# Gates on ScalarE, a second routing with PSUM operands, and weight decoding moved into the last stage

## The chip, the cores and the metric

The kernel runs on one core of one Trainium2 chip, as one program. The metric is the device time of one launch in microseconds (us); lower is better. The kernel before takes 538.42 us, the median of three runs (537.2 to 539.23). The core's engines are TensorE (PE in the profile, its weight loads PEld), VectorE (DVE), ScalarE (ACT), GpSimd (POOL) and SyncE (SP), which here only issues DMAs.

## The reference

Three blocks follow each other, all in float32:

```python
# 1. attention: B=2, H=8, S=576, D=64
scores = (1/sqrt(D)) * rotate(q) @ rotate(k).T      # rotary embedding
attn = exp(scores - max); attn /= sum(attn) + 1e-9
x = (attn @ v)  reordered to (1152 tokens, 512)

# 2. routed experts: 8 experts, 512 -> 1024 -> 512, one expert per token
logits = x @ w_gate + modality_bias[modality_id]
e_idx = argmax(logits); gate_w = softmax(logits)[e_idx]
out[mask] = gate_w[mask] * (relu(x[mask] @ w1[e]) @ w2[e])      # for each expert e

# 3. dense block: 512 -> 2048 -> 512
h = out @ w_in
y = (h * tanh(softplus(h))) @ w_out
```

## The kernel before, in words

**Precision.** Products are made in a reduced float format with a correction: each operand is split into a high part (ScalarE copies it, for instance `whi`, `xh`, `hh`, `w2h`) and a low part (VectorE or POOL subtracts: `wlo`, `xl`, `hl`, `w2l`), and each product takes three matmuls: high by high, high by low, low by high.

**Attention** handles the 16 heads in an order that a planner (`Plan`) writes out ahead of time from estimated durations. Its X tiles collect the attention output per token; `LG` collects the gate logits of each head.

**Routing** (`routing(b, bank)`) runs once for each half of the tokens (b = 0, 1): a long chain of small VectorE operations turns the logits into the expert of each token, its place among the tokens of that expert, the table of the expert tiles (`tbl`, `te`) and the number of extra tiles (`nx`). Each token's row, with its gate value in an extra column, is scattered to DRAM by five indirect DMAs on POOL. For b = 0 the chain is interleaved with attention, and its intermediate results lie in a corner of a PSUM bank (`side`, `near`, `cur["rtile"]`); for b = 1 it runs after attention, and they lie in SBUF. `merge_extra` then joins the two tables of extra tiles, and `nx` is loaded into a register on the engines (`values_load`).

**Expert stage.** Four main tiles, (0, 0), (0, 1), (1, 0), (1, 1), of 304 tokens each. `moe_g` multiplies a tile's rows by their gates (line 630), `moe_x` transposes them on TensorE and splits them, and `moe_tile` makes eight products of the first matrix (12 matmuls each; ScalarE writes `hh`, VectorE `hl`, line 706) and four of the second (24 matmuls each; ScalarE writes Y, line 731). The next tile's gates are issued at the start of the second matrix, its transposes after the second of these four products. The tile's weights come in eight chunks through SP's queue (line 577), are split by ScalarE (line 585) and POOL (line 590), and a chunk is loaded when an older one has been split. A loop over extra tiles, which runs zero or more times, stands between the first two tiles and the last two.

All of this is written as generators, which yield ahead of each operation the engine and an estimated duration; for TensorE each matmul is one yield. Their consumers set the order. While routing 1 runs, `pump` issues an amount of expert matmuls for each VectorE yield of the routing, and afterwards `drive` steps through the rest and slips in a decode step at every so-many yields:

```python
if y[0] == "dve":
    pump(P["rq"][(i > 9) + (i > 20)])        # P["rq"] = (0.45, 0.47, 0.2)
...
nq_[0] += 1                                   # one TensorE yield
if nq_[0] % (3 * every) == 0:                 # every = P["dec"][0..2]
    decode(1, limit)
```

**Decoding.** The last stage's weights (16 blocks, f = 0 to 15, each 128 x 1024) come as 64-bit words, 1 MB per block, and three VectorE integer operations per block rebuild the 32-bit values (lines 1188, 1193, 1198). After a block's third step the load of block f + 2 is issued on SP's queue (line 1181; there are two buffers). Near the end of tile (0, 1) a "quiet" mark stops decoding for 48 yields.

**Last stage.** The dense block takes the token columns in two groups, first 640 columns in two pieces of 320, then 512 in two pieces of 256. For each of 16 weight blocks and each piece there is one unit `h` (12 matmuls, line 1346), then tanh, square and copy on ScalarE, a reciprocal (line 1368) and a product (line 1369) on VectorE, a high part on ScalarE and a low part on POOL (line 1386), and the output products `o` (line 1403). The three PSUM banks of `h` are reused in turn, so a unit waits for the line-1369 product of the third unit before it. What is not yet decoded is decoded here, in a fixed place about four units ahead of its use:

```python
m = 2 * q
if q < FC2:
    for z in range(3):
        at2(m - 4.05 + 0.6 * z, lambda n=3 * q + z + 1: decode(n - nd[0]))
```

`decode` does nothing for steps that are done. [...]

Of the kernel before, what the change touches and what calls it, by code (L numbers as in the profile page):

```python
# [10 lines left out]
F32 = mybir.dt.float32  # L11
F32R = mybir.dt.float32r
I32 = mybir.dt.int32
AF = mybir.ActivationFunctionType
ALU = mybir.AluOpType
AX = mybir.AxisListType
PSUM = bass.MemoryType.PSUM
# [3 lines left out]
DM = H * D  # L21
# [7 lines left out]
XC = DM  # L29
# [6 lines left out]
FC2 = F2 // 128  # L36

Q = {'r0': 2.45, 'rd': 2.0, 'tanh': 1.06, 'rec': 1.1, 'hi': 2.2, 'lo': 2.38, 'o': 3.86}
P = {'sd': (3,), 'dl': (10, 20), 'qd': (2, 3), 'alt': (0.1, 4), 'd0': 41, 'vl': 9, 'c': (-145.0, 22.5, -2.0), 'w3': 3, 'rq': (0.45, 0.47, 0.2), 'dec': (5, 5, 5), 'rl': 3, 'ah': 0, 'eps': 0.05, 'slack': 0.1}
K = {'ld': -22.67, 'prep': (-24.92, -22.38, -23.33, -27.14, -20.49, -7.62), 'sc': (-8.42, -3.18, 1.68, 1.67, 2.84, 10.44, 1.99, 8.05, 9.75), 'max': (-2.26, -5.46, -1.21, -1.85, 5.06, 8.41, 4.71, 11.42, 13.72), 'exp': (-3.19, 1.66, 6.32, 3.7, 13.26, 11.14, 14.6, -2.87, 25.74), 'tr': (0.69, 2.1, 2.56, 2.68, 5.53, 7.5, 8.45, 9.85, 10.88, 11.85, 15.56, 16.66, 16.92, 19.98), 'hi': (-3.91, -0.31, 2.51, 3.62, 4.25, 4.9, 5.01, 5.32, 7.26, 9.77, 13.56, 14.12, 14.6, 15.66), 'lo': (0.77, 1.83, 5.61, 6.34, 6.67, 7.32, 10.02, 10.73, 12.18, 13.92, 13.94, 14.62, 17.33, 18.02), 'pv': (7.08, 7.84, 10.5, 10.69, 14.13, 14.25, 14.32, 15.96, 18.04, 20.31, 21.03, 22.86, 23.97, 25.61), 'evac': (14.53, 9.65, 6.27, 25.13), 'rec': (-4.7, -0.45, 4.11, 12.71), 'fmm': (4.53, -3.79, 16.24, 17.22), 'norm': (15.5, 16.11, 26.18, 35.69)}  # L40

QT = [(0, 128), (128, 128), (256, 64), (320, 128), (448, 128)]
# [31 lines left out]
class Plan:  # L74
# [39 lines left out]
    def pick(self, e):  # L114
        best, lines = None, set()
        for o in self.todo[e][:40]:
# [8 lines left out]
            if best is None or t < best[0] - 1e-9:  # L125
                best = (t, o)
            if t <= self.free[e] + P["eps"]:
                break
# [40 lines left out]
    def run(self):  # L169
# [3 lines left out]
        while any(self.todo.values()):  # L173
            best = None
            for e in self.todo:
                c = self.pick(e)
                c = c and (c[0], 1, c[1])
                for o in self.alt[e][:4]:
# [4 lines left out]
                    t = max(t, self.free[e])  # L183
                    if (c is None or t + o[4] - P["alt"][0] <= c[0]) and t + o[4] + P["alt"][1] < end:
                        c = (t, 1, o)
                for st in self.streams:
                    if st["next"][0] != e:
                        continue
                    t = self.start(st)
                    if c is None or t + (st["next"][1] - P["slack"] if e in st["low"] else 0.0) <= c[0]:  # L190
                        c = (t, 0, st)
# [19 lines left out]
def moe_kernel(ctx: ExitStack, tc: tile.TileContext, aps, out):  # L211
    nc = tc.nc
# [87 lines left out]

    regs = {}
    tbl = {}
    scat, nxs, tes = [], [], []

    def routing(b, bank):
        t = lambda sh, nm, dt=F32: rp.tile(sh, dt, tag=nm, name=f"{nm}{b}")
        side = b == 0
        room = [0]

        def near(sh, nm):  # L310


            if not side:
                return t(sh, nm)
            n = 1
            for x in sh[1:]:
                n *= x
            o = room[0]
            room[0] += n
            v = cur["rtile"][0:sh[0], o:o + n]  # L320
            if len(sh) == 3:
                v = v.rearrange("p (a b) -> p a b", b=sh[2])
            return v

        V = nc.vector
# [4 lines left out]
            out=lg, in_=LG[b].rearrange("p j h e -> p j e h"),  # L330
# [15 lines left out]
            out=val, in0=lg, scalar=0.0, in1=iota8[:, 0:1, :].to_broadcast(sh),  # L346
            op0=ALU.is_ge, op1=ALU.mult,
# [46 lines left out]
        if not side:  # L394
# [8 lines left out]
            out=pos, in_=pz.rearrange("p (e j) -> p j e", j=5), axis=AX.X, op=ALU.add  # L403
# [5 lines left out]
        for j, (_, qn) in enumerate(QT):  # L409
            yield "pool", 1.07, False  # L410
            sc = nc.gpsimd.indirect_dma_start(
                out=scratch, out_offset=bass.IndirectOffsetOnAxis(ap=row[:qn, j:j + 1], axis=0),
                in_=X[b][:qn, j], in_offset=None,
# [9 lines left out]
        n0 = t([1, NE], "n1")  # L423
# [5 lines left out]
            out=n1, in0=ce, scalar=float(T), in1=n0, op0=ALU.is_gt, op1=ALU.add  # L429
        )  # L430
        if side:
# [5 lines left out]
            out=qi, data0=n1, data1=zero[0:1, :NE], initial=0.0, op0=ALU.add, op1=ALU.add  # L437
# [7 lines left out]
            out=st, in0=s0, scalar=float(-T), in1=base[0:1, 0:n:5], op0=ALU.mult, op1=ALU.add  # L445
# [5 lines left out]
            out=nx, in0=qi[:, NE - 1:NE], scalar1=-2.0, scalar2=None, op0=ALU.add  # L451
        )
        tv = iotat[0:1, 0:ns]
        if b:
# [3 lines left out]
                out=tv[:, 0:2], in0=iotat[0:1, 0:2], scalar1=nx, scalar2=None, op0=ALU.add  # L458
# [3 lines left out]
                out=tv[:, 2:ns], in0=iotat[0:1, 2:ns], scalar1=nxs[0], scalar2=-2.0,  # L462
                op0=ALU.subtract, op1=ALU.add,
# [3 lines left out]
        if side:  # L467
# [4 lines left out]
            out=lt, in0=qi[:, None, :].to_broadcast(s8),  # L472
            in1=tv[:, :, None].to_broadcast(s8), op=ALU.is_le,
        )
        te = t([1, ns, 2], f"te{b}")
        tm = near([1, ns, 2], "tm") if side else te
# [7 lines left out]
            out=lt, in0=iota8[0:1, 0:1, :].to_broadcast(s8),  # L484
            in1=e8[:, :, None].to_broadcast(s8), op=ALU.is_equal,
# [8 lines left out]
            out=cs, in0=tv, scalar=float(T), in1=cs, op0=ALU.mult, op1=ALU.add  # L494
# [4 lines left out]
            out=tm[:, :, 1], in0=cs, scalar1=s1, scalar2=o1, op0=ALU.mult, op1=ALU.add  # L499
# [3 lines left out]
            out=tm[:, :, 1], in0=tm[:, :, 1], scalar1=0.0, scalar2=float(ROWS - T),  # L503
            op0=ALU.max, op1=ALU.min,
# [3 lines left out]
            out=tm[:, :, 0], in0=tm[:, :, 0], scalar1=float(NE - 1), scalar2=None, op0=ALU.min  # L508
        )
        if side:  # L510
            yield "dve", 0.12, True
            V.tensor_copy(te, tm)
        tes.append(te)
        tbl[b] = ti = const.tile([1, 2, 2], I32, name=f"tbl{b}")
        yield "dve", 0.12, True
        V.tensor_copy(ti, te[:, 0:2])

    def merge_extra(nx):

        V = nc.vector  # L520
        n0, n1 = NS[0] - 2, NS[1] - 2
        sh = [1, n0, 2]
        m = rp.tile([1, n0], F32, tag="mm", name="mm")
        yield "dve", 0.12, True
        V.tensor_scalar(
            out=m, in0=iotat[0:1, 0:n0], scalar1=nxs[0], scalar2=None, op0=ALU.is_lt
        )
        d = rp.tile(sh, F32, tag="md", name="md")
        yield "dve", 0.12, True
        V.tensor_tensor(out=d, in0=tes[0][:, 2:], in1=tes[1][:, 2:2 + n0], op=ALU.subtract)  # L530
        yield "dve", 0.12, True
        V.tensor_tensor(out=d, in0=d, in1=m[:, :, None].to_broadcast(sh), op=ALU.mult)
        yield "dve", 0.12, True
        V.tensor_tensor(
            out=tes[1][:, 2:2 + n0], in0=tes[1][:, 2:2 + n0], in1=d, op=ALU.add
        )
        ei = const.tile([1, n1, 2], I32, name="ei")
        yield "dve", 0.12, True
        V.tensor_copy(ei, tes[1][:, 2:])
        yield "dve", 0.12, True  # L540
        V.tensor_tensor(out=nx, in0=nxs[0], in1=nxs[1], op=ALU.add)
        nc.sync.dma_start(out=extra.rearrange("(o r) c -> o r c", o=1), in_=ei)
# [36 lines left out]
    def split_chunk(k, i):  # L579
# [6 lines left out]
        lo = pool.tile([128, 1024], F32R, tag="wlo", name=f"wlo{k}_{i}", bufs=n)  # L586
        dve = k == (0, 0) and i in P["sd"]
        yield ("dve", 1.14, False) if dve else ("pool", 2.3, False)
# [4 lines left out]
    class Feed:  # L593
# [6 lines left out]
        def loads(self, n):  # L600
            self.want = max(self.want, min(n, len(self.seq)))
            while self.nl < min(self.want, self.ns + (2 if len(wpool) == 1 else P["w3"])):
                k = self.seq[self.nl][0]
# [20 lines left out]
    def moe_g(k):  # L624

        x = xrow[k]
        gated.add(k)
        yield "dve", 1.2, True
        for i, (_, rn) in enumerate(TCH):
            nc.vector.tensor_scalar(  # L630
                out=x[:rn, i, 0:DM], in0=x[:rn, i, 0:DM],
                scalar1=x[:rn, i, XC + 1:XC + 2], scalar2=None, op0=ALU.mult,
            )

    def moe_x(k, bank):
# [23 lines left out]
    def moe_tile(k, feed, bank):  # L659

        at_ = feed.tiles.index(k)
        ah = 4 if len(wpool) == 1 else 2 + P["w3"] + P["ah"]
        kk = at_ * NCH
# [440 lines left out]
    cur = {}  # L1104
# [8 lines left out]
    def route(b):  # L1113
        yield from routing(b, lambda: cur["rbank"]())
        if b:
            tile_rows(b)
# [107 lines left out]

    with ExitStack() as mctx:
        sctx = m1ctx.enter_context(ExitStack())
        ps_m = mctx.enter_context(tc.tile_pool(name="ps_m", bufs=8, space=PSUM, reuse_waits="tile"))
        n_m = [0]

        def bank3():  # L1230
# [26 lines left out]
        for i, y in enumerate(chain(route(1), merge_extra(nx))):  # L1257
            if i in P["dl"]:
                dec_load(len(wr))
            if y[0] == "dve":  # L1260
                pump(P["rq"][(i > 9) + (i > 20)])
# [44 lines left out]
        def pool(name, bufs, **kw):  # L1306
            return ectx.enter_context(
                tc.tile_pool(name=name, bufs=bufs, reuse_waits="tile", **kw)
            )

        w2p, yp, gp, op = (
            pool(n, b) for n, b in (("w2p", 1), ("yp", 1), ("gp", 3), ("op", 5))
        )
# [222 lines left out]
```

## Time and profile before

| what | value |
|---|---|
| median of three runs | 538.42 us |
| the profiled execution's own time | 542.5 us |
| its span, first to last instruction | 540.4 us |
| mean granted TensorE clock | 0.969 |
| TensorE busy | 489.1 us (91%) |
| VectorE busy | 439.6 us (81%) |
| POOL busy | 362.2 us (67%) |
| ScalarE busy | 326.1 us (60%) |

The profile is one execution of the program on the chip. Busy times of engines lie beside each other and do not add up to the span. Matmuls are pipelined and their ends are modelled, so a busy TensorE need not be TensorE at its best. Times in the rows count from the first instruction. The chain that ended last is made of TensorE from 358 us on; ahead of that, from the expert stage to the first part of the last stage, it changes between TensorE and VectorE.

### The profile page before, as it was taken

What the parts mean: (1) busy time and instruction counts of PE and PEld (TensorE: products, weight loads), DVE (VectorE), ACT (ScalarE), POOL (GpSimd) and SP (SyncE); (2) the same over time, 40 slices, a digit from 0 to 9 for tenths busy, and PEclk for the clock granted to TensorE, in tenths of its full rate; (3) what the DMA queues carried; (4) which work ended last, traced back from release to release, by engine and by line L of the source; (5) the groups of instructions that cost most, each with busy time, mean ns of one, the idle gap of its engine ahead of it and who ended that gap; (6) DMA issues with size and microseconds to landing.
All of it is one profiled execution on the core that took longest, in us unless ns stands there. A gap on an engine that the chain in (4) does not pass through costs nothing.

```text
span 540.4 us, 9170 instructions
## 1 busy us (share of the span) xinstructions
PE 489.1 (91%) x3152; PEld 452.1 (84%) x3152; DVE 439.6 (81%) x639; ACT 326.1 (60%) x735; POOL 362.2 (67%) x350
## 2 busy tenths in 40 slices
PE   0599999998999897989589978999999999999996
PEld 0589999987899697988589977889999999999994
DVE  5968989887898779895399878998879986877773
ACT  2357888765788343442344526777665668777673
POOL 4669999979842338583464946667556767977664
PEclk9999999999999688998899989999999999999999
DMA  7877777856742555875485745000000000100001
GB/s 225 116 200 193 195 194 189 214 161 173 190 108 85 192 216 168 322 279 213 125 300 208 280 191 157 0 1 0 2 1 0 2 0 21 60 19 1 1 2 78
DMA packets 23939, 68.67 MB, mean 127 GB/s; under 512 B 5330, under 2 KB 9618, under 8 KB 21842
## 3 DMA queue, kind: packets, MB, share of 16 engines
q1 hardware_dynamic: 21602, 62.70, 38.8%
q0 software_dynamic: 1456, 4.74, 2.3%
q10 hardware_dynamic: 832, 0.61, 0.4%
q8 instruction: 27, 0.44, 0.3%
q14 instruction: 22, 0.18, 0.1%
HBM read 48.77 MB, written 5.99 MB: 101 GB/s over the span
## 4 chain that ended last, share of the span: by engine, by line
PE 38%; DVE 10%; ACT 2%; issue 1%; DMA 1%; POOL 0%; POOLq 0%; SPq 0%
PE h L1346 16%; PE o L1403 16%; PE mm L681 6%; DVE ta L1368 2%; DVE wc L1193 2%; DVE wc L1188 2%; DVE yl L1294 2%; DVE wc L1198 1%; DMA wraw(1, 0)_3_3822<-in_w_dram 1%; DVE hl(1, 1)_4160 L706 1%; DVE hl(1, 0)_3821 L706 0%; ACT w2h L1329 0%; PE mm L647 0%; DVE ta L1369 0%; POOL out_dram L1413 0%
## 5 line engine op out<-in xcount | busy, mean ns | idle before, releaser
L1368 DVE RECIPROCAL ta<-ta 128x320 f32<-128x320 f32 (+1 forms) x64 | 124.8, 1950 | 29.4 <-ACT ta L1361 28.5
L1403 PE MATMUL o<-w2h,g 128*128 128x512 f32 x288 | 100.0, 394 | 0.0
L1386 POOL TENSOR_TENSOR g<-ta,g 128x320 fp32r<-128x320 f32 (+1 forms) x63 | 53.4, 847 | 62.5 <-issue 40.6
L1330 POOL TENSOR_TENSOR w2l<-wc,w2h 128x512 fp32r<-128x512 f32 x64 | 84.6, 1343 | 4.8 <-ACT w2h L1329 4.8
L1346 PE MATMUL h<-yh,w2h 128*128 128x320 f32 (+1 forms) x256 | 75.9, 296 | 1.7 <-DVE ta L1369 1.7
L1346 PE MATMUL h<-yl,w2h 128*128 128x320 f32 (+1 forms) x256 | 75.8, 296 | 1.1 <-DVE yl L1294 1.1
L1346 PE MATMUL h<-yh,w2l 128*128 128x320 f32 (+1 forms) x256 | 75.9, 296 | 0.6 <-POOL w2l L1330 0.6
L876 PE MATMUL sc<-sk,sq 128*128 128x288 f32 (+1 forms) x320 | 59.3, 317 | 16.3 <-DVE sq L803 10.5
L893 ACT ACTIVATE pexp<-sc,nm 128x576 f32<-128x576 f32 x72 | 53.3, 741 | 29.2 <-DVE nm L886 23.3
L926 ACT ACTIVATE ph<-pt 128x512 fp32r<-128x512 f32 (+2 forms) x112 | 54.4, 509 | 14.0 <-PE pt L906 13.3
L876 PEld LDWEIGHTS sc<-sk,sq 128*128 128x128 f32 (+1 forms) x320 | 47.8, 194 | 18.0 <-ACT sk L800 10.5
L1403 PEld LDWEIGHTS o<-w2h,g 128*128 128x128 f32 x288 | 54.0, 188 | 10.3 <-POOL g L1386 0.3
L886 DVE TENSOR_REDUCE nm<-sc 128x1 f32<-128x576 f32 x72 | 53.4, 752 | 11.2 <-PE sc L876 10.0
L1403 PE MATMUL o<-w2l,g 128*128 128x512 f32 x144 | 56.7, 394 | 0.0
L906 PE MATMUL pt<-ident,pexp 128*128 128x128 f32 (+1 forms) x360 | 53.9, 277 | 0.7 <-DVE mx L337 0.3
L947 PE MATMUL av<-ph,vhl 128*128 128x256 f32 (+1 forms) x160 | 52.0, 340 | 2.6 <-DVE av L386 0.5
L1346 PEld LDWEIGHTS h<-yh,w2h 128*128 128x128 f32 x256 | 48.2, 188 | 5.0 <-DVE ta L1369 2.4
L932 DVE TENSOR_TENSOR pl<-pt,ph 128x512 fp32r<-128x512 f32 (+1 forms) x80 | 49.0, 628 | 4.0 <-ACT ph L926 3.4
L1346 PEld LDWEIGHTS h<-yl,w2h 128*128 128x128 f32 x256 | 48.1, 188 | 3.9 <-DVE yl L1294 1.4
L1346 PEld LDWEIGHTS h<-yh,w2l 128*128 128x128 f32 x256 | 48.2, 188 | 0.8 <-POOL w2l L1330 0.8
L1357 ACT ACTIVATE ta<-h 128x320 f32<-128x320 f32 (+1 forms) x64 | 25.8, 404 | 34.4 <-PE h L1346 30.3
L906 PEld LDWEIGHTS pt<-ident,pexp 128*128 128x128 f32 (+1 forms) x360 | 42.4, 138 | 2.9 <-PE sc L876 1.1
(445 smaller groups left out, 1279.4 us busy)
## 6 DMA issues: line engine op xcount, KB each, us to landing
wr<-in_wio_dram SPq DMA_DIRECT2D x16, 1024.0 KB, 4.8
xs<-in_qk_dram SPq DMA_DIRECT2D x15, 576.0 KB, 5.5
sk<-ab SPq DMA_DIRECT2D x30, 288.0 KB, 4.1
sq<-ab SPq DMA_DIRECT2D x30, 144.0 KB, 2.4
vraw<-in_v_dram SPq DMA_DIRECT2D x16, 160.0 KB, 2.5
scratch<-zero SPq DMA_DIRECT2D x2, 612.8 KB, 16.6
tabs<-in_rope_dram SPq DMA_DIRECT2D x2, 288.0 KB, 5.1
xs<-in_qk_dram ACTq DMA_DIRECT2D x2, 288.0 KB, 4.6
```

The costliest lines, as they stand in the source:

```text
L876: nc.tensor.matmul(t[:m, hf, :NC2], lhsT=sq[:, c:c + m], rhs=sk[:, z, hf * NC2:(hf + 1) * NC2], start=(z == 0), stop=(z == 1),)
L886: nc.vector.tensor_reduce(out=nm[n, j], in_=sc[n, j][:, :, :NC2], axis=AX.XY, op=ALU.max, negate=True)
L893: nc.scalar.activation(out=pe, in_=sc.pop((n, j))[:, :, :NC2], func=AF.Exp, bias=nm.pop((n, j)), accum_out=st[n, hf][:, i:i + 1],)
L906: nc.tensor.transpose(out=t[:kn, o:o + 128], in_=pexp[n, j][:, k0:k0 + kn], identity=ident)
L926: nc.scalar.activation(out=block(ph, n, hf, kts, slice(0, kn)), in_=psum(n, hf, kts, kn), func=AF.Copy)
L932: nc.vector.tensor_tensor(out=block(pl, n, hf, kts, slice(0, 128)) if kn == 128 else block(ph, n, hf, kts, slice(64, 128)), in0=psum(n, hf ...
L947: nc.tensor.matmul(av[n, hf][:, :u.nq], lhsT=vhl[n][:, kt].rearrange("p a d -> p (a d)"), rhs=src[:, kt, u.at:u.at + u.nq], start=(kt == 0 ...
L1330: nc.gpsimd.tensor_tensor(out=lo[:, cs], in0=w[:, cs], in1=hi[:, cs].bitcast(F32), op=ALU.subtract)
L1346: nc.tensor.matmul(ps[:, :w], lhsT=wt[:, c], rhs=m[g, i][:, c], start=(n == 0), stop=(n == 11))
L1368: nc.vector.reciprocal(out=ta, in_=ta)
L1386: eng.tensor_tensor(out=gt[q][1][:, o:o + w], in0=tas.pop((q, i))[:, :w], in1=gt[q][0][:, o:o + w].bitcast(F32), op=ALU.subtract,)
L1403: nc.tensor.matmul(acc[g, t], lhsT=a[:, s], rhs=b, start=(f == 0 and z == 0), stop=(f == FC2 - 1 and z == 2),)
```

## The change

- `P['dec']` goes from (5, 5, 5) to (8, 8, 8): `drive` slips in a decode step at every 24th TensorE yield in place of every 15th.
- `side` is true for both halves: routing 1 keeps its intermediate results in PSUM too, in a bank of its own (`ps_r`), and takes the branches that were routing 0's (the scan and the sum read the matmul result in PSUM and are no longer yields of their own; copies of `n1` and `tm` to SBUF are added). The ring `ps_m` has 7 banks.
- `merge_extra` reads the table of routing 1 from PSUM (`tms[1]`).
- `moe_g` multiplies by the gates on ScalarE (an activation with the gate column as its scale) and no longer on VectorE.

```diff
-P = {... 'dec': (5, 5, 5), ...}
+P = {... 'dec': (8, 8, 8), ...}
...
-        side = b == 0
+        side = True
...
+        tms.append(tm)
...
-        V.tensor_tensor(out=d, in0=tes[0][:, 2:], in1=tes[1][:, 2:2 + n0], op=ALU.subtract)
+        V.tensor_tensor(out=d, in0=tes[0][:, 2:], in1=tms[1][:, 2:2 + n0], op=ALU.subtract)
...
         V.tensor_tensor(
-            out=tes[1][:, 2:2 + n0], in0=tes[1][:, 2:2 + n0], in1=d, op=ALU.add
+            out=tes[1][:, 2:2 + n0], in0=tms[1][:, 2:2 + n0], in1=d, op=ALU.add
         )
...
-        yield "dve", 1.2, True
+        yield "act", 1.5, True
         for i, (_, rn) in enumerate(TCH):
-            nc.vector.tensor_scalar(
-                out=x[:rn, i, 0:DM], in0=x[:rn, i, 0:DM],
-                scalar1=x[:rn, i, XC + 1:XC + 2], scalar2=None, op0=ALU.mult,
+            nc.scalar.activation(
+                out=x[:rn, i, 0:DM], in_=x[:rn, i, 0:DM], func=AF.Copy,
+                scale=x[:rn, i, XC + 1:XC + 2],
             )
...
-        ps_m = mctx.enter_context(tc.tile_pool(name="ps_m", bufs=8, space=PSUM, reuse_waits="tile"))
+        ps_m = mctx.enter_context(tc.tile_pool(name="ps_m", bufs=7, space=PSUM, reuse_waits="tile"))
+        ps_r = mctx.enter_context(tc.tile_pool(name="ps_r", bufs=1, space=PSUM, reuse_waits="tile"))
+        cur["rtile"] = ps_r.tile([128, 512], F32, name="rt1")
```

## Rows read from the trace of the kernel before

**Rows 1.** Busy us (and count) per stretch: PE, PEld, DVE, ACT, POOL, clock, DMA share, GB/s:

```profile
205.80:328.20 122.40, 109.91 (x708) 105.18 (x708) 98.01 (x92) 49.54 (x85) 74.39 (x30) 0.93 0.63 231
328.20:358.70 30.50, 27.12 (x153) 23.84 (x151) 29.28 (x26) 20.69 (x49) 19.27 (x16) 1.00 0.14 40
358.70:439.20 80.50, 80.47 (x449) 72.88 (x450) 70.65 (x55) 54.25 (x120) 53.35 (x48) 1.00 0.00 1
```

**Rows 2.** Waits, 185 to 358 us: who waited for whom: us, times, longest:

```profile
PE mm L681 <- DVE xrow(0, 1)_2741 L630: 3.2, 1, 3.2
PE mm L681 <- DVE hl(1, 1)_4160 L706: 2.8, 2, 2.2
PE mm L681 <- DVE hl(1, 0)_3821 L706: 1.8, 1, 1.8
PE mm L681 <- DVE hl(0, 1)_3128 L706: 1.4, 2, 1.1
PE h L1346 <- DVE yl L1294: 1.1, 1, 1.1
PE mm L647 <- DVE xrow(1, 0)_3192 L630: 1.0, 1, 1.0
PE mm L360 <- DVE oh L355: 0.9, 1, 0.9
```

**Rows 3.** Stretches as in rows 1, behind the 3.2 us wait:

```profile
207.00:210.40 3.40, 3.40 (x16) 3.40 (x16) 3.37 (x2) 0.00 (x0) 3.40 (x4) 0.51 0.20 78
210.40:213.80 3.40, 3.40 (x26) 3.40 (x26) 3.37 (x2) 1.36 (x2) 1.57 (x1) 0.98 0.85 254
```

**Rows 4.** Single lines: duration min/median/max in ns; first half at 110, second at 190:

```profile
L355 DVE TENSOR_TENSOR oh<-iota,av x1: 225/225/225, 110.0 to 110.0; 128x40 f32<-128x40 f32 x1
L355 DVE TENSOR_TENSOR oh<-iota,ix x1: 2351/2351/2351, 184.3 to 184.3; 128x40 f32<-128x40 f32 x1
L436 DVE TENSOR_TENSOR_SCAN av<-av,zero x1: 170/170/170, 125.4 to 125.4; 1x8 f32<-1x8 f32 x1
L436 DVE TENSOR_TENSOR_SCAN qi<-n,zero x1: 2336/2336/2336, 197.2 to 197.2; 1x8 f32<-1x8 f32 x1
L399 DVE TENSOR_TENSOR av<-av,oh x1: 207/207/207, 114.1 to 114.1; 128x40 f32<-128x40 f32 x1
L399 DVE TENSOR_TENSOR pz<-pz,oh x1: 199/199/199, 195.1 to 195.1; 128x40 f32<-128x40 f32 x1
```

**Rows 5.** Decode lines as in rows 4; then a gates group (busy us, mean ns):

```profile
L1193 DVE SCALAR_TENSOR_TENSOR wc<-wr,wc x16: 1207/1748/5957, 207.1 to 423.8; 128x1024 int32<-128x1024 int32 x16
L1188 DVE TENSOR_SCALAR wc<-wr x16: 676/686/2516, 206.4 to 419.9; 128x1024 int32<-128x1024 int32 x16
...
L630 DVE TENSOR_SCALAR xrow(1, 0)_3192<-xrow(1, 0)_3192 128x512 f32<-128x512 f32 (+1 forms) x3 | 5.4, 1867 | 0.0
```

**Rows 6.** ScalarE groups by line: busy us, mean ns, idle before and its releaser:

```profile
L1329 ACT ACTIVATE w2h<-wc 128x512 fp32r<-128x512 f32 x16 | 9.1, 616 | 0.0
...
L893 ACT ACTIVATE pexp<-sc,nm 128x576 f32<-128x576 f32 x72 | 53.3, 741 | 29.2 <-DVE nm L886 23.3
```

**Rows 7.** Waits of SP's own queue, 185 to 335 us (as in rows 2):

```profile
SPq L1181 <- DVE wc L1198: 66.4, 13, 8.1
```

**Rows 8.** Chain that ended last, in order of time: start us, us, what:

```profile
369.14 1.77 PE h L1346 x12
...
432.20 1.77 PE h L1346 x12
```

**Rows 9.** VectorE's timeline in the last stage: start us, us, line, operation:

```profile
385.99 1.22 DVE L1476 CAST idi<-idf 128x9 int32<-128x9 f32 x1
...
419.93 1.37 DVE L1188 TENSOR_SCALAR wc<-wr 128x1024 int32<-128x1024 int32 x1
...
428.65 2.15 DVE L1368 RECIPROCAL ta<-ta 128x320 f32<-128x320 f32 x1
430.83 0.49 DVE L1369 SCALAR_TENSOR_TENSOR ta<-ta,h 128x320 f32<-128x320 f32 x1
```

More of the change, by code (lines that the diff above doesn't have):

```diff
@@ L38 @@
 Q = {'r0': 2.45, 'rd': 2.0, 'tanh': 1.06, 'rec': 1.1, 'hi': 2.2, 'lo': 2.38, 'o': 3.86}
-P = {'sd': (3,), 'dl': (10, 20), 'qd': (2, 3), 'alt': (0.1, 4), 'd0': 41, 'vl': 9, 'c': (-145.0, 22.5, -2.0), 'w3': 3, 'rq': (0.45, 0.47, 0.2), 'dec': (5, 5, 5), 'rl': 3, 'ah': 0, 'eps': 0.05, 'slack': 0.1}
+P = {'sd': (3,), 'dl': (10, 20), 'qd': (2, 3), 'alt': (0.1, 4), 'd0': 41, 'vl': 9, 'c': (-145.0, 22.5, -2.0), 'w3': 3, 'rq': (0.45, 0.47, 0.2), 'dec': (8, 8, 8), 'rl': 3, 'ah': 0, 'eps': 0.05, 'slack': 0.1}
 K = {'ld': -22.67, 'prep': (-24.92, -22.38, -23.33, -27.14, -20.49, -7.62), 'sc': (-8.42, -3.18, 1.68, 1.67, 2.84, 10.44, 1.99, 8.05, 9.75), 'max': (-2.26, -5.46, -1.21, -1.85, 5.06, 8.41, 4.71, 11.42, 13.72), 'exp': (-3.19, 1.66, 6.32, 3.7, 13.26, 11.14, 14.6, -2.87, 25.74), 'tr': (0.69, 2.1, 2.56, 2.68, 5.53, 7.5, 8.45, 9.85, 10.88, 11.85, 15.56, 16.66, 16.92, 19.98), 'hi': (-3.91, -0.31, 2.51, 3.62, 4.25, 4.9, 5.01, 5.32, 7.26, 9.77, 13.56, 14.12, 14.6, 15.66), 'lo': (0.77, 1.83, 5.61, 6.34, 6.67, 7.32, 10.02, 10.73, 12.18, 13.92, 13.94, 14.62, 17.33, 18.02), 'pv': (7.08, 7.84, 10.5, 10.69, 14.13, 14.25, 14.32, 15.96, 18.04, 20.31, 21.03, 22.86, 23.97, 25.61), 'evac': (14.53, 9.65, 6.27, 25.13), 'rec': (-4.7, -0.45, 4.11, 12.71), 'fmm': (4.53, -3.79, 16.24, 17.22), 'norm': (15.5, 16.11, 26.18, 35.69)}
@@ L302, in moe_kernel @@
     tbl = {}
-    scat, nxs, tes = [], [], []
+    scat, nxs, tes, tms = [], [], [], []
     def routing(b, bank):
         t = lambda sh, nm, dt=F32: rp.tile(sh, dt, tag=nm, name=f"{nm}{b}")
-        side = b == 0
+        side = True
         room = [0]
```

## The prediction

> **What bounds the kernel now.** I read the page first (TensorE is the busiest engine, VectorE the next), then busy time by stretch, then the waits, then single lines. By stretch [rows 1], TensorE is busy 109.91 of 122.40 us in the expert stage, at a mean clock of 0.93, and 80.47 of 80.50 us in the first column group of the last stage. There anything that stays behind TensorE is free, until VectorE (70.65 of the 80.50 us) no longer keeps up. In the expert stage TensorE has holes, and the waits [rows 2] name who ends them: VectorE, nearly each time. TensorE waits 2.8, 1.8 and 1.4 us for `hl`, the low part of the hidden layer, which VectorE computes between decode steps; 1.0 us for the gated rows of tile (1, 0); 0.9 us for the one-hot matrix of the second half's routing; 1.1 us for `yl` as the last stage begins. The 3.2 us row names a gate operation that starts just before TensorE goes on; by the code it is the register load of the count of extra tiles, which needs the end of the routing. The skip over the extra-tile loop also holds everybody up, and the change does not touch it.
>
> [...]
>
> **How much work moves.** The driver of the experts decodes one step at every 15th TensorE yield before, at every 24th after. Counted through the generators: the first half has three transposing stages of 4 yields and two tiles of 192, 396 in all, of which one goes in attention and 93 in the routing's pump, so 302 are driven; then 196 and 192: 690. 690/15 gives 46 steps, less the 4 that fall behind "quiet": 42, so 14 of 16 weights. After: of the routing's VectorE yields three go that are pumped at 0.47 (memset, scan, sum) and two come at 0.2 (copies). The pump's sum falls from 13.03 to 12.02 us, by 1.01/0.1275 = 8 matmuls. So 698 are driven; 698/24 gives 29, less 2: 27 steps, 9 weights. Seven weights, not two, are decoded in the last stage.
>
> **Part A, routing in PSUM.** Two steps of the second half's routing were held up: the one-hot compare took 2351 ns, against 225 in the first half, whose operands lie in PSUM, and the scan 2336 against 170 [rows 4]; POOL was in a weight split (line 590) both times. With PSUM operands I expect the first half's times. The scan gives 2.17 us; the compare gives only the 0.9 us that TensorE waited, since VectorE then idled until TensorE had caught up. Two added copies take back 0.3. So the routing ends about 2.8 us earlier. But 8 matmuls that ran ahead of its end (8 x 0.131 = 1.0) now come behind it: 1.7 us is the best end. The other end: its last steps (table cast, merge product) still have SBUF operands, and the split of chunk 4 now stands behind the five scatters in POOL's queue instead of ahead of them, and so beside these steps; one such hold-up of 2.2 leaves +0.5. What that split itself loses is covered by the stall that remains. I take -1.3, near the best end, since few steps are exposed. The hole does not vanish, so its stretch of low clock stays.
>
> [...]
>
> **Part B, gates on ScalarE and fewer decode steps among the experts.** The gates of tile (1, 0) took 5.4 us on VectorE [rows 5], again beside POOL. The trace has no such operation on ScalarE; a plain one of 128x512 takes 0.62 us, one with a per-row operand and 576 columns 0.74 [rows 6]: 1.8 to 2.2 us per tile, and I take 1.8, the nearer shape. For three tiles it lies in ScalarE's queue ahead of a tile's first Y evacuation, for which ScalarE waits anyway; behind it are queued only that evacuation and the next weight split. Cost 0; without that cover 1.8 us per tile. The first tile's gates fall at the end of attention, where ScalarE comes free about when VectorE did: 0, at worst their own 1.8. Gained are the 1.0 us and one stretch of low clock.
>
> The `hl` waits: the second kind of decode step takes 1.75 us in the median and up to 5.96 [rows 5], and a tile's first product has 96 yields, so 96/15 = 6.4 steps fell into it; now 4 do. Then VectorE has caught up before the next step comes, and an `hl` is late by one step at most, which the 24 matmuls of the next product cover but for a little. So 2.8 + 1.8 + 1.4 = 6.0 us go, and two stretches of low clock. B is -(6.0 + 1.0 + 3 x 1.3) = -10.9 at best; in tile (1, 1) a step falls right ahead of the last `hl`, so I leave 1.0: -9.9. If the holes only shrink and the clock still falls, -5. Late next is nothing on TensorE's path: the DMA share is 0.63 among the experts [rows 1], and five loads of 1 MB go from there to the last stage, where it is 0.00. In SP's queue such loads waited 66.4 us in all for decode steps [rows 7], with expert weights queued behind them, so that eases too. The ring of banks goes from 8 to 7: a bank is wanted again 7 x 12 matmuls, some 11 us, later; 0.
>
> **Part C, entry of the last stage.** Two decode steps ran just ahead of the last `yl`. Without them I take -1.0 of the 1.1 us wait [rows 2]; the ends are 0 and -1.1.
>
> **Part D, five more weights decoded in the last stage.** 18 units of TensorE work take 432.20 - 369.14 = 63.06 us [rows 8], and a weight is two units: 7.01. VectorE needs for a weight's three steps, with the two reciprocals and gate products between them, 428.65 - 419.93 = 8.72 us [rows 9]. It falls behind 1.71 per weight. Two weights in a row were carried by the slack: the last gate product ended at 430.83 + 0.49 = 431.32, and the unit that reuses its bank began at 432.20, with 0.88 to spare. Now five more weights, and the cast of 1.22 falls into the full stretch: 5 x 1.71 + 1.22 - 0.88 = 8.9 us of TensorE waiting, all on the path. If the first step, which took 1.37 beside a POOL operation, takes its median of 0.69 [rows 5], a weight takes 8.04 and the sum is 5.5; if the second takes its median of 1.75 for 1.22, 9.25 and 11.6. I take the measured pattern, 8.9. Afterwards VectorE catches up, and nothing is given back.
>
> **Sum.** A -1.3, B -9.9, C -1.0, D +8.9: -3.3 us. The profiled execution took 542.5 us (span 540.4), 4.1 above the median of 538.4; I apply the difference to the median: 535.1.
>
> **Rivals.** (1) VectorE's steps in the last stage go unhindered, as POOL has gaps once TensorE waits: D is 5.5, the time 531.7. For it: most first steps took 0.69. Against it: in the pattern at hand the step did collide. (2) Slower: VectorE bounds seven weights at its high price, and TensorE, waiting in each, has its clock lowered there too: 11.6 + 3 x 1.3 = 15.5, against gains of 12.2: +3.3, 541.7. It decides from D above 12.2. For it: the low stretches follow holes of 1 to 3 us. Against it: a slower TensorE lets VectorE catch up, and after the 1.1 us hole at the last stage's entry the clock stayed at 1.00 [rows 1]. (3) The holes among the experts are not the decode steps' doing; another wait (weights, POOL's splits) takes their place, B is -5 and C 0: +2.6, 541.0. Against it: neither ends a wait of TensorE worth naming there. [...]
>
> **How the numbers follow.** Forecast 0.45, rivals 0.20, 0.15, 0.12, 0.08. About 0.5%, 2.7 us, is what a measurement can tell from no change. The forecast's own range is 532.5 to 537.5; 0.27 of its 0.45 lies beyond -2.7. Faster 0.27 + 0.20 = 0.47; same 0.18 + 0.08 + half of (3), 0.06 = 0.32; slower 0.15 + 0.06 = 0.21. For 8 in 10 I take 529 (A, B, C at their best ends and D at 5.5 make -8.2) to 541.5 (where the two high rivals lie).
>
> **What would show it.** 27 decode steps ahead of the last stage, no `hl` wait over 1 us, three stretches of low clock less, the last stage's first unit some 12 us earlier; then VectorE without idle time over seven weights of about 8.7 us, and TensorE waiting some 9 us in all for gate products. Wrong would be: a last stage as long as before, or experts that gain under 6 us.

## The result, and the profile of the changed kernel

The changed kernel takes 533.16 us in the median of four runs (531.03 to 533.77), the kernel before 538.83 us beside it (537.2 to 544.01). The ratio is 0.9894, with a 95% interval of 0.9861 to 0.9928: faster by 5.7 us, where 3.3 were forecast.

The profiled execution of the changed kernel took 533.38 us, near its median; that of the kernel before took 542.5, some 4 us above its own. The two profiles so lie 9.1 us apart where the medians lie 5.7 apart. A difference of 3 us between single profiles is not read as an effect below, unless rows say what it consists of. One such difference stands at the start: from 180 us to 193.4 the granted clock of the kernel before was 0.50, in the changed kernel only to 187.0; and in two later kernels whose routing is that of the kernel before the matmuls there were slow for 3.4 us alone, one every 0.25 us (gates and decoding changed, 184.8 to 188.1 us; late steps spread, 187.9 to 191.3).

Taking the first matmul of each tile, and the first `h` of the last stage, as marks, the two profiles divide so (us):

| from, to | before | after | difference |
|---|---|---|---|
| tile (0,0), (0,1) (with the routing) | 40.0 | 38.1 | -1.9 |
| tile (0,1), (1,0) | 39.4 | 34.3 | -5.1 |
| tile (1,0), (1,1) | 34.1 | 31.1 | -3.0 |
| tile (1,1), first `h` | 31.8 | 26.7 | -5.1 |
| first `h`, end of span | 212.4 | 219.7 | +7.3 |

The remaining 0.9 us was there before the first tile began, in a part that the change does not touch.

Busy time by stretch of the changed kernel, with the columns of [rows 1]. The first three lines are tiles (0,1), (1,0) and (1,1), the fourth the entry of the last stage, the fifth its first column group:

```profile
219.90:254.20 34.30, 29.20 (x207) 28.06 (x205) 13.28 (x18) 17.16 (x29) 22.78 (x9) 0.97 0.67 231
254.20:285.30 31.10, 31.10 (x205) 30.21 (x206) 17.38 (x20) 14.82 (x25) 20.77 (x9) 0.93 0.70 240
285.30:312.00 26.70, 26.70 (x194) 26.70 (x194) 21.95 (x22) 14.44 (x26) 17.81 (x8) 1.00 0.49 179
312.00:341.80 29.80, 27.34 (x155) 24.03 (x154) 27.47 (x25) 20.78 (x50) 18.57 (x16) 1.00 0.12 36
341.80:422.30 80.50, 73.92 (x406) 65.55 (x407) 78.48 (x63) 47.99 (x105) 53.03 (x42) 1.00 0.19 66
```

The same three tiles of the kernel before:

```profile
222.70:262.10 39.40, 31.52 (x206) 29.55 (x204) 25.86 (x25) 15.85 (x26) 23.05 (x9) 0.95 0.66 244
262.10:296.20 34.10, 32.27 (x205) 31.14 (x206) 29.86 (x28) 13.01 (x22) 17.42 (x8) 0.91 0.63 223
296.20:328.00 31.80, 29.01 (x194) 28.34 (x194) 26.11 (x28) 14.60 (x27) 22.34 (x8) 0.95 0.63 237
```

Read TensorE's column against the length. Tiles (1,0) and (1,1) have no hole left: 31.10 of 31.10 and 26.70 of 26.70 us. The number of matmuls is the same (205, 194), yet the busy time shrinks: 32.27 to 31.10, 29.01 to 26.70. In part that is the clock, whose column rises. In part it is what a hole does to the matmuls beside it. Two of the holes of tile (1,1) in the kernel before (start us, us, in brackets the wait):

```profile
311.66 0.30 PE L681 MATMUL mm<-hh(1, 1)_4159,wlo(1, 1)_4_4242 128*128 128x304 f32 x1
311.80 0.30 PE L681 MATMUL mm<-hh(1, 1)_4159,whi(1, 1)_4_4240 128*128 128x304 f32 x1
312.69 0.41 PE L681 MATMUL mm<-hl(1, 1)_4160,whi(1, 1)_4_4240 128*128 128x304 f32 x1 [0.59 <-DVE hl(1, 1)_4160 L706]
312.94 0.30 PE L681 MATMUL mm<-hh(1, 1)_4159,wlo(1, 1)_4_4242 128*128 128x304 f32 x1
...
316.00 0.41 PE L681 MATMUL mm<-hl(1, 1)_4160,whi(1, 1)_4_4240 128*128 128x304 f32 x1 [2.20 <-DVE hl(1, 1)_4160 L706]
316.25 0.39 PE L681 MATMUL mm<-hh(1, 1)_4159,wlo(1, 1)_4_4242 128*128 128x304 f32 x1
316.43 0.46 PE L681 MATMUL mm<-hh(1, 1)_4159,whi(1, 1)_5_4280 128*128 128x304 f32 x1
316.69 0.46 PE L681 MATMUL mm<-hl(1, 1)_4160,whi(1, 1)_5_4280 128*128 128x304 f32 x1
```

In an unbroken row a matmul starts every 0.14 us and lasts 0.30, so neighbours overlap. The matmul behind the hole of 0.59 us overlaps with none, lasts 0.41, and the next follows after 0.25: the two starts that should be 0.14 us each take 0.89 and 0.25, so 0.86 us are lost, 0.27 more than the profile calls idle. After the second hole the clock falls (0.52 from 316.2 to 319.6 us), and matmuls start every 0.25 us.

In the last stage it is the other way: VectorE's busy time rises from 70.65 [rows 1] to 78.48 of 80.50 us, and TensorE, full before, is busy 73.92.

TensorE's waits, 185 to 480 us, for comparison with [rows 2], and below them the wait of the kernel before for gate products (185 to 360 us; it has no later one):

```profile
PE h L1349 <- DVE ta L1372: 8.5, 8, 1.5
PE mm L682 <- DMA wraw(1, 0)_3_3807<-in_w_dram: 5.1, 1, 5.1
PE mm L682 <- DVE hl(0, 0)_2662 L707: 2.2, 1, 2.2
PE mm L682 <- POOL wlo(0, 0)_4_2788 L591: 1.0, 1, 1.0
PE h L1349 <- POOL w2l L1333: 0.6, 1, 0.6
PE h L1349 <- DVE yl L1297: 0.2, 1, 0.2
```

```profile
PE h L1346 <- DVE ta L1369: 1.7, 2, 1.0
```

The waits for `hl` and for gated rows are gone (the 2.2 us row names an `hl`, but as in the kernel before it is the register load of the count of extra tiles; the 5.1 us row is the skip over the extra-tile loop). `yl` is down to 0.2. One wait is new among the experts, 1.0 us for the split of chunk 4, and one large one stands in the last stage: 8.5 us for gate products, 6.8 more than before. The clock of tile (1,0) stays at 0.93 without a hole in it, since the low stretch that the skip leaves behind is longer here, 6.8 us for 3.4 (251.8 to 258.6 us, at 0.50).

The routing's two steps that were held up [rows 4] are short now:

```profile
L355 DVE TENSOR_TENSOR oh<-iota,rt x1: 232/232/232, 183.8 to 183.8; 128x40 f32<-128x40 f32 x1
...
L436 DVE TENSOR_TENSOR_SCAN rt<-rt,zero x1: 158/158/158, 192.6 to 192.6; 1x8 f32<-1x8 f32 x1
```

The gates take ScalarE about what the nearer row of [rows 6] said, three instructions in 1.9 us:

```profile
L631 ACT ACTIVATE xrow(1, 0)_3182<-xrow(1, 0)_3182 128x512 f32<-128x512 f32 (+1 forms) x3 | 1.9, 709 | 0.0
```

And VectorE in the last stage, from one weight's first decode step to the next one's (start us, us, line):

```profile
376.74 1.37 DVE L1189 TENSOR_SCALAR wc<-wr 128x1024 int32<-128x1024 int32 x1
378.03 2.14 DVE L1371 RECIPROCAL ta<-ta 128x320 f32<-128x320 f32 x1
380.20 0.49 DVE L1372 SCALAR_TENSOR_TENSOR ta<-ta,h 128x320 f32<-128x320 f32 x1
380.61 1.22 DVE L1194 SCALAR_TENSOR_TENSOR wc<-wr,wc 128x1024 int32<-128x1024 int32 x1
381.74 2.15 DVE L1371 RECIPROCAL ta<-ta 128x320 f32<-128x320 f32 x1
383.92 0.49 DVE L1372 SCALAR_TENSOR_TENSOR ta<-ta,h 128x320 f32<-128x320 f32 x1
384.33 1.22 DVE L1199 SCALAR_TENSOR_TENSOR wc<-wr,wc 128x1024 int32<-128x1024 int32 x1
385.46 1.38 DVE L1189 TENSOR_SCALAR wc<-wr 128x1024 int32<-128x1024 int32 x1
```

385.46 - 376.74 = 8.72 us with no idle time, for two units that TensorE does in 7.01. It is the number of [rows 9], and so is the first step's slow form, 1.37.

### The profile page after: what moved, and what is told of

Same layout as the page of the kernel before. It is cut to its first block, busy times and chain, and to the rows that moved or that the text cites. A ratio compares the mean times of both kernels' runs of the same rounds, so it can differ in the third digit from the quotient of the medians.

```text
span 531.7 us, 9169 instructions
## 1 busy us (share of the span) xinstructions
PE 484.3 (91%) x3152; PEld 448.2 (84%) x3152; DVE 412.4 (78%) x629; ACT 333.0 (63%) x747; POOL 366.1 (69%) x350
## 5 line engine op out<-in xcount | busy, mean ns | idle before, releaser
L1389 POOL TENSOR_TENSOR g<-ta,g 128x320 fp32r<-128x320 f32 (+1 forms) x63 | 57.4, 911 | 64.4 <-issue 27.4
L907 PE MATMUL pt<-ident,pexp 128*128 128x128 f32 (+1 forms) x360 | 55.1, 282 | 0.7 <-DVE mx L337 0.3
L1383 ACT ACTIVATE g<-ta 128x320 fp32r<-128x320 f32 (+1 forms) x64 | 27.9, 436 | 34.7 <-DVE ta L1372 34.6
L907 PEld LDWEIGHTS pt<-ident,pexp 128*128 128x128 f32 (+1 forms) x360 | 43.5, 140 | 2.7 <-PE sc L877 1.1
```

The lines of the kernel that those rows point to most:

```text
L907: nc.tensor.transpose(out=t[:kn, o:o + 128], in_=pexp[n, j][:, k0:k0 + kn], identity=ident)
L1389: eng.tensor_tensor(out=gt[q][1][:, o:o + w], in0=tas.pop((q, i))[:, :w], in1=gt[q][0][:, o:o + w].bitcast(F32), op=ALU.subtract,)
```

## The experiments

Twelve kernels ran, in three groups, each beside runs of the kernel before on the same chip. Ratios are to that kernel; a difference in us is a median less the median beside it.

**Each part by itself.** Decoding slower, alone:

```diff
-'dec': (5, 5, 5)
+'dec': (8, 8, 8)
```

> The kernel before with only the decode rate changed (every 24th TensorE yield). First theory (fewer decode steps close the holes among the experts, and five more weights in the last stage cost about 8 us): the experts gain 9 to 11 us with the clock, the last stage loses 8, so 2 to 4 us faster than before, 535 to 537. Rival (the gain of the whole change comes from routing and gates, and moved decoding is paid back in full): 0 to 3 us slower than before, 539 to 542.

534.95 us against 539.56, ratio 0.9922 [0.9896, 0.9948]. Every `hl` wait is gone, and the 1.0 us wait for the gates of tile (1,0) as well, although the gates are still on VectorE: both were VectorE's delay behind decode steps. Its last stage is as long as the changed kernel's (220.2 against 219.7 us).

The gates on ScalarE, alone (the kernel before with the change's new lines of `moe_g`):

```diff
-        yield "dve", 1.2, True
+        yield "act", 1.5, True
...
-            nc.vector.tensor_scalar(
+            nc.scalar.activation(
```

> The kernel before with only the gates moved to ScalarE. First theory: the 1.0 us hole at the transposes of tile (1, 0) goes and one stretch of low clock with it, 2 to 3 us faster, 535.5 to 537; the waits for hl stay. Rival (the gates on VectorE only shift decode steps, and the hl waits take the hole's place): within 1 us of before.

535.96 us, ratio 0.9941 [0.9913, 0.9969]: 3.6 us by themselves. The profile keeps the `hl` waits (3.2 us in tile (1,1), 1.9 in (1,0), 1.3 in (0,1)); what shrank is the stretch from tile (0,1) to (1,0), 36.1 us for 39.4, the one with the slow gates of [rows 5], where the 1.0 us wait for them is gone. The stretch from tile (0,0) to (0,1) shrank too, 38.6 us for 40.0; what did that was not separated from the clock at its start.

The routing with operands in PSUM, alone (all of the diff but the gates and `dec`):

> The kernel before with only the second half's routing in PSUM (ring of 7 banks). First theory: the two held-up steps go, and the pump runs 8 matmuls less ahead of the routing's end; as the profile of the whole change shows a first unit of tile (0, 1) that is 2.8 us earlier, 2 to 3 us faster, 535.5 to 537. [...]

543.43 us, ratio 1.0083 [1.005, 1.0116]: slower by 3.9, where 2 to 3 us faster were expected. The profiled execution is no typical one: it took 539.75 us, the shortest of ten. TensorE's waits of this kernel, 175 to 330 us:

```profile
...
PE mm L682 <- DVE hl(1, 1)_4158 L707: 2.9, 2, 2.1
PE mm L682 <- DVE hl(1, 0)_3817 L707: 2.3, 1, 2.3
PE mm L682 <- POOL wlo(0, 0)_4_2788 L591: 1.9, 1, 1.9
PE mm L682 <- DVE hl(0, 0)_2662 L707: 1.9, 1, 1.9
PE mm L682 <- POOL wlo(0, 1)_2_3130 L591: 1.9, 1, 1.9
```

Two of them are new, both for POOL's splits: chunk 4 of tile (0,0) and chunk 2 of tile (0,1), 1.9 us each. Added up, the parts' -4.6, -3.6 and +3.9 make -4.3, and together they give -5.7; with intervals of 1.4 to 1.8 us each way, the two can't be told apart.

**The change with one part undone.** The changed kernel with decoding as before (`'dec': (5, 5, 5)`):

> The changed kernel with the decode rate of before (14 weights decoded among the experts). First theory: routing and gates alone, 4 to 6 us faster than before, 533 to 535, so about as fast as the whole change. Rival: routing and gates are the whole gain and decoding is paid back with a loss: 7 us or more faster than before, under 532, so faster than the whole change.

541.15 us, ratio 1.0038 [1.001, 1.0067], above both bands. With decode steps as dense as before, the change is worth nothing. The waits for `hl` are back (3.1 us in tile (0,1), 2.3 in (1,0)), and that for chunk 4 is 2.7.

The kernel before with `dec` at 8 and the gates on ScalarE, its routing untouched:

> The change without its routing part: gates on ScalarE and every 24th yield, routing in SBUF as before. If the parts add up (decode alone -4.2, gates alone -3.2, routing alone +4.5), 531 to 533 and 1 to 3 us faster than the whole change. Second theory (routing in PSUM costs time only where VectorE is full of decode steps, by the place at which the steps fall, and helps a little otherwise): 533 to 535, the same as the whole change or up to 2 us slower.

533.56 us against 540.5, ratio 0.9878 [0.9856, 0.99]. That is the changed kernel's ratio within both intervals: in this company the routing in PSUM gives nothing that can be measured.

**The price in the last stage.** The changed kernel with one operation instead of three per weight for the weights from the tenth on (it leaves out their other two operations; the loads stay):

```diff
+        late = f >= 9
...
+        if not late:
             nc.vector.scalar_tensor_tensor(
```

> The changed kernel, with one VectorE operation instead of three for each of the seven weights that are decoded in the last stage (those weights come out wrong; loads and waits stay). First theory (the last stage loses about 8 us because VectorE needs 8.7 us per weight against 7.0 of TensorE): with one operation VectorE needs under 6 us, the waits for gate products go, 7 to 8 us faster than the changed kernel, 525 to 526.5. Rival (the last stage would be as long anyway: loads of 1 MB in it, or the clock): within 2 us of the changed kernel.

525.49 us, ratio 0.9726 [0.9705, 0.9748], 7.7 us under the changed kernel by the medians and further by the ratios (15.0 against 5.7 us under the kernel before); between the profiles the last stage is 8.2 us shorter (211.5 for 219.7). TensorE is busy throughout the first column group again, and waits 1.7 us in all for gate products:

```profile
341.80:422.30 80.50, 80.50 (x451) 72.81 (x450) 68.11 (x56) 54.08 (x120) 50.70 (x49) 1.00 0.18 66
```

**The hole at the routing.** In the changed kernel the split of chunk 4 stands behind the five scatters in POOL's queue, and the routing ends when too few matmuls have been pumped. More of them beside the routing's later steps:

```diff
-'rq': (0.45, 0.47, 0.2)
+'rq': (0.45, 0.72, 0.18)
```

> The changed kernel with the routing's pump at (0.45, 0.72, 0.18), so that as many matmuls run ahead of the routing's end as before and the split of chunk 4 stands ahead of the five scatters in POOL's queue again. If that order is what opens the 1.0 us wait for the split and prolongs the stretch of low clock behind it: 1 to 3 us faster than the changed kernel, 530 to 532, no wait for wlo(0, 0)_4. Rival (the chain then waits for more expert products, as before, and its end comes later by as much): within 1 us of the changed kernel.

530.07 us, ratio 0.9821 [0.9798, 0.9844], some 4 us better than the changed kernel. Tile (0,0) takes 34.8 us for 38.1; the wait for chunk 4 is gone. The stretch of low clock behind the hole, changed kernel first (three stretches, then a stretch of the new kernel and the one after it; columns as in [rows 1], the second fence TensorE alone):

```profile
200.80:204.20 3.40, 2.41 (x9) 2.18 (x9) 3.09 (x2) 0.28 (x1) 3.40 (x2) 0.50 0.35 104
204.20:207.60 3.40, 3.40 (x15) 3.40 (x15) 1.88 (x2) 2.24 (x4) 1.20 (x2) 0.52 0.85 288
207.50:210.90 3.40, 3.40 (x26) 3.40 (x26) 0.00 (x0) 2.02 (x4) 2.69 (x2) 1.00 0.61 237
```

```profile
200.40:203.80 3.40, 3.40 (x17) 0.54 0.32 107
203.80:207.20 3.40, 3.40 (x25) 0.95 0.89 302
```

Nine and fifteen matmuls in the changed kernel's two low stretches, against seventeen and twenty-five in the new one's low stretch and the one after it: the second hole, of 1.0 us, came while the clock was low from the first, and the clock stayed down for twice as long.

The same share of matmuls in the routing-only kernel, and in the kernel before:

> The routing's operands in PSUM alone (decode every 15 items, gates on VectorE), with the larger share of matmuls beside the routing (0.72, 0.18). If that part alone was slower (543.4) because the routing ends earlier and leaves TensorE at the split of chunk 4 behind the scatters, 4 us come back: 539 to 540, no slower than before. If it was slower because decode steps and low halves collide on VectorE in tile (0,1), the time stays: 542 to 544.

539.71 us against 539.1, ratio 1.0004 [0.9977, 1.003]. As the first theory had it, the routing alone is no longer slower. The wait for chunk 4 is gone, though one of 1.3 us for chunk 5 has come.

> The kernel before with nothing changed but the share of matmuls beside the second half's routing (0.72, 0.18). If the 3 to 4 us that this share gave in the changed kernel need the shorter routing, because the routing's chain ends last in the kernel before anyway: within 1.5 us of before, 537.5 to 540.5. If the share is worth the same by itself: 535 to 536.

548.18 us, ratio 1.015 [1.0108, 1.0193]: 9 us slower, which neither theory held. VectorE and POOL, at the end of the routing:

```profile
204.86 0.47 DVE L630 TENSOR_SCALAR xrow(0, 1)_2738<-xrow(0, 1)_2738 48x512 f32<-48x512 f32 x1
205.26 0.15 DVE L530 TENSOR_TENSOR md<-te,te 1x16 f32<-1x16 f32 x1
205.44 0.16 DVE L532 TENSOR_TENSOR md<-md,mm 1x16 f32<-1x16 f32 x1
205.64 5.27 DVE L534 TENSOR_TENSOR te<-te,md 1x16 f32<-1x16 f32 x1
...
206.23 2.34 POOL L590 TENSOR_TENSOR wlo(0, 0)_5_2826<-wraw(0, 0)_5_2760,whi(0, 0)_5_2824 128x1024 fp32r<-128x1024 f32 x1
208.53 2.34 POOL L590 TENSOR_TENSOR wlo(0, 0)_6_2924<-wraw(0, 0)_6_2822,whi(0, 0)_6_2922 128x1024 fp32r<-128x1024 f32 x1
...
210.94 0.17 DVE L539 CAST ei<-te 1x32 int32<-1x32 f32 x1
...
211.77 0.59 PE L681 MATMUL mm<-hh(0, 0)_2658,whi(0, 0)_4_2762 128*128 128x304 f32 x1 [8.13 <-DVE nxi L541]
```

The larger share pulls the gates of tile (0,1) in among the routing's last steps, so they come about a microsecond later than in the kernel before (204.47 for the same L534, 0.16 us long there). That is enough to meet POOL's two splits (by the profile's times L534 starts 0.6 us ahead of them and ends with the second), and sixteen elements take 5.27 us. TensorE waits 8.1 us for the register load.

**Spreading the late steps.** Gates on ScalarE, `dec` at 7 and the late decode steps one per unit from unit 9.3 on (the cast moved to 28.6):

```diff
-                    at2(m - 4.05 + 0.6 * z, lambda n=3 * q + z + 1: decode(n - nd[0]))
+                    at2(9.3 + 3 * (q - 10) + z, lambda n=3 * q + z + 1: decode(n - nd[0]))
```

> Gates on ScalarE, routing as before, every 21st yield (30 steps, 10 weights among the experts), and in the last stage one decode step per unit, from unit 9 on, with the cast of the token numbers moved behind them. First theory (VectorE has 1.8 us free per weight from unit 9 on, unused so far, and the loss is only that the seven weights come too closely): nearly all of the 8 us come back, 526 to 529. Rival (each step costs the last stage its length wherever it lies): 531 to 534.

531.93 us against 540.5, ratio 0.984 [0.9821, 0.986]. Against gates and `dec` 8 with the bunched steps (533.56) it brings back some 2 of 8 us; the number lies in the rival's band. With a step in each unit VectorE is busy 72.25 of 73.30 us (its column is the third) and from unit 16 to 28 sets the pace, 46.5 us for twelve units, 3.87 each for TensorE's 3.50: some 18 steps were too many.

```profile
343.70:417.00 73.30, 71.47 (x383) 60.75 (x383) 72.25 (x57) 45.14 (x100) 51.39 (x40) 1.00 0.16 58
```

The changed kernel with the larger share, decoding by phase (every 24 yields in the first product, every 15 in the second) and the rest spread over units 9.3 to 26.9:

```diff
-                if nq_[0] % (3 * every) == 0:
-                    decode(1, limit)
+                nq_[0] += 1 / (3 * cur["ph"])
+                if nq_[0] >= 1:
+                    nq_[0] -= 1
+                    decode(1, limit)
...
+                    at2(9.3 + 17.55 * (3 * q + z - n0) / (47 - n0), lambda n=3 * q + z + 1: decode(n - nd[0]))
```

> The changed kernel, with the larger share of matmuls in the second half's routing (0.72, 0.18), with decode steps among the experts more often where no low halves of activations are made (every 15 matmul items there, every 24 in the first matrix), so that 35 of 48 steps lie ahead of the last stage, and with the remaining 13 steps spread evenly over units 9.3 to 26.9 of the last stage. If the last stage loses only because VectorE's steps are bunched from unit 16 on: 13 steps of about 1.3 us are 16.9 us, and 18 units leave about 0.92 us each, 16.6 us, so nearly all of the 8 to 9 us comes back: 522 to 525. If the extra 9 steps among the experts bring back the waits for low halves, half of that is lost: 526 to 528. If a step's price in the last stage is paid wherever it lies, 530 less 8 x 13/22 at most: 526 to 527, with the loss spread over units 9 to 27.

527.17 us, ratio 0.979 [0.9747, 0.9832], the best of the versions that decode every weight whole. From unit 9 on nothing is lost: TensorE is busy 77.28 of 77.30 us with 13 steps beside it.

```profile
343.40:420.70 77.30, 77.28 (x430) 69.95 (x431) 75.22 (x61) 53.25 (x117) 56.44 (x47) 1.00 0.12 42
```

The time that misses from the 522 to 525 that this should have given stands at the entry, where VectorE has decode steps between the last `yl`:

```profile
PE h L1352 <- DVE yl L1300: 4.4, 2, 3.4
...
PE h L1352 <- DVE ta L1375: 1.0, 1, 1.0
```

The matmuls behind them are slow (fourteen of `h` in 4.11 us from 315.57, where twelve later take 1.76), and the entry takes 34.7 us for the changed kernel's 29.8. So the number, 527, lay in the band of the second theory, but not for its reason: no wait for `hl` came back. Nor is it the third theory's reason, as units 9 to 27 lost nothing. With the same spread and decoding every 18 yields throughout:

> As the run before it, but one decode step every 18 matmul items throughout the experts (36 of 48 steps ahead of the last stage, 12 spread in it). If the place of a step among the experts matters, VectorE falls behind with the low halves in the first matrices and TensorE waits for them: 2 to 4 us slower than the run before it, 525 to 528. If only the number of steps counts, the same as it within 1 us.

528.5 us, ratio 0.9807 [0.9771, 0.9843]. One `hl` wait of 0.6 us, and 4.1 us for `yl`. The two can't be told apart: where the steps lie among the experts matters little at this density.

## Why the prediction held, and where it didn't

**How much work moves.** Twenty-seven steps ahead of the last stage and seven weights in it came out as counted: VectorE's timeline has seven first steps in the last stage, from 358.59 to 411.65. The last stage's first unit came 16.0 us earlier, where some 12 were named.

**D, forecast +8.9 (5.5 to 11.6): right.** From the first `h` to the end the changed kernel is 7.3 us longer, C's 1.0 us gain included: 8.2 to 8.3 for D. The waits show the mechanism (8.5 us for gate products, 1.7 of them there before, so 6.8 more), VectorE's 8.72 us a weight the size, and taking the operations away shows that it is VectorE's work and not the loads, which remained: 7.7 us by the medians, 8.2 between the profiles, 9.3 by the ratios. The 1.4 us beside the waits are busy time: from the first `h` to the end TensorE is busy 205.19 us for 203.78, with the same 1201 matmuls and the clock high in both, and six waits are new, with a longer matmul behind each as in the rows above. The forecast made all of D waiting. Rival (2) fell: the holes of 1.5 us in the last stage left the clock at 1.00. Rival (1) needed the first step at 0.69 us; six of the seven took 1.37 or 1.38, as in the pattern that the forecast chose.

**C, forecast -1.0: right.** The `yl` wait went from 1.1 to 0.2 us.

**B, forecast -9.9: right in its mechanism, too small.** The three tiles hold 13.2 us less between the profiles. Of that 7.4 us are TensorE's idle time (7.88 to 5.10, 1.83 to 0, 2.79 to 0), where 6.0 were forecast: the 1.0 that I left in tile (1,1) went too, and the skip over the extra-tile loop, which the change does not touch, was 0.4 shorter. The other 5.8 us are busy time for the same matmuls (2.3, 1.2 and 2.3). About 4.0 of them are clock, where three stretches of 1.3 us, 3.9, were forecast (1.3 us is what the ten matmuls by which the two lines of [rows 3] differ take at 3.40/26 = 0.131 us each, the price that part A has for its 8 matmuls too): the three at 248, 282 and 316 us are gone, 3.4 us each, with a matmul every 0.25 us for 0.14 (1.5 us lost in each), and the one behind the skip costs 0.7 more. So the price of a low stretch held. The term that the sum did not have is the rest, 1.8 us. A hole takes about 0.27 us more than the profile calls idle, as shown above, and six are gone: an estimated 1.6. Not all of the 13.2 us can be trusted, since that profile of the kernel before lies above its median; but the runs say the same: decoding and gates without the routing gave -6.9 us, where B, C and D were to make -2.0. Rival (3) fell with it: slower decoding alone closed every `hl` hole. The gate wait goes in two ways, where I had one: with the gates on ScalarE, and by slower decoding with the gates left on VectorE. The gates alone were worth 3.6 us, more than the wait and one low stretch, 2.3, that the sum gave them.

**A, forecast -1.3 (-1.7 to +0.5): the steps right, the sentence on chunk 4 wrong.** Compare and scan came out at the first half's times, and the routing ended 6.4 us earlier (198.33 for 204.76, 0.9 of it an earlier start). Not all of this is the routing's doing: counted from the first matmul of tile (0,0), its end comes after 22.1 us in the kernel before, 20.5 with gates and decoding changed and the routing in SBUF, 16.5 in the changed kernel. It was not worth 1.3 us in this kernel (against the kernel without it, 0.4 gained by the medians and 1.2 lost by the differences to the kernel before, which can't be told from none), and by itself, under dense decoding, it cost 3.9. The step that failed is "What that split itself loses is covered by the stall that remains". It is not covered: the register load's hole closes at 199.55, the split starts at 199.58, and TensorE stands again for 1.0 us, with the clock low from the first hole. "So its stretch of low clock stays" was half of it: the stretch doubled, from 3.4 to 6.8 us. With more matmuls beside the routing, 3 to 4 us come back. That the chain ends 4.0 us earlier than with the routing in SBUF and gains so little shows what bounds this part: not the chain alone, but what was pumped in front of TensorE, which the sum counted as 8 matmuls, and where chunk 4's split stands.

**The errors partly cancel.** B, C and D gave 4.9 us more than forecast, A 0.9 to 2.5 less; so the sum, -5.7 for -3.3, came nearer than its terms, and that is luck. For A the outcome is no gain that can be measured, the case that has 0.08 of the chances. Operands in PSUM cost one step 8 ns: the product of 40 columns took 207 ns in the second half with PSUM operands, as in the first, and 199 without [rows 4]; the compare took 232 ns, and 225 in the first half, both with an operand in PSUM.

**Open.** Why the routing in PSUM under dense decoding also lengthens tile (0,1), by 1.7 us, with POOL's split of chunk 2 late, was not separated; and as that profile is of the shortest of ten runs, most of the 3.9 us of the median stands in no trace here. That more pumped matmuls bring them back is shown by the medians alone. In the best version the entry's `yl` wait was not removed.

## What to carry to other kernels

Before moving work from a stage where it makes holes to one where it has none, count the receiver's slack per unit: here 13 steps spread evenly over 18 units cost nothing there, 18 cost 0.4 us a unit over the twelve units in which VectorE had fallen behind, and 21 bunched from unit 14 on 8 us. The price of a hole was here its length, 1.5 us more where a low stretch of 3.4 us followed it, and 0.27 us for the matmul behind it. A chain that becomes shorter helps only if the work kept beside it is dealt out anew: the same larger share gave 3 to 4 us with the short routing and cost 9 with the long one. And parts of a change should be timed each alone and with the others, since one that costs 3.9 us alone was free here.

## What the runs showed of the hardware that was not expected

- A VectorE operation on 16 elements in SBUF took 5.27 us when it ran into two weight splits on POOL, 2.34 us each, back to back, and 0.16 us when it ended before them. Here the hold-up lasted until POOL's second split ended (210.91 us, the split 210.87), not for one POOL operation as in [rows 4] (the compare to 186.66 us, the split beside it to 186.58; the scan to 199.54, the split to 199.51). The one-hot compare with one of its operands in PSUM took 0.23 us although it ran within such a split (183.8 us, the split 183.30 to 185.66); with both in SBUF it had taken 2.35. Held up were thus the compare, the scan and this operation, each with two tensors in SBUF; but a decode step with one input in SBUF was held up as well (L1189, 3.35 us at 201.50, beside splits until 204.29; 0.69 at 358.59, with POOL idle). What decides between them was not shown.
- With a second hole of 1.0 us while the clock was still low (0.50), the low stretch was 6.8 us long; without that hole it was 3.4 (0.54). Holes of 1.5 us, one every 8.7 us in the last stage, came with the clock high and left it at 1.00.
- A hole cost TensorE 0.27 us beyond its idle time, since the matmul behind it overlapped with none ahead and lasted 0.41 us for 0.30. A busy time that shrinks at the same number of matmuls is therefore not clock alone.
